# A gated mix of linear attention and expert lookup on one core: the subtracted feature and key moved to the end, one copy's order changed, and the seam, tile 5 and the drain put in another order

## The chip, the cores and the metric

The kernel is one program on one core of a Trainium2 chip. The core has a matrix engine (TensorE, PE; its weight loads are shown apart as PEld), a vector engine (VectorE, DVE), an activation engine (ScalarE, ACT), a general engine (GpSimd, POOL) and a queue engine (SyncE, SP), each with its own instruction queue worked off in order. They meet through semaphores. SBUF is the working memory of 128 partitions, PSUM the memory in which products are summed, in banks of 128 x 512 32-bit numbers. POOL does not read PSUM in this kernel. The metric is the device time of one execution in microseconds (us), the median of several runs.

## The reference

For 2048 tokens x of width 512, the output is `g*a + (1-g)*b`, with `g = sigmoid(sum(x*gate_w))`.

```
# a: linear attention, 32 heads of 16, feature map = two softmaxes per head
q, k, v = split(x @ wqkv)
pq, pk  = per head: q @ w_phi, k @ w_phi                # 16 features a head
phi(p)  = concat(softmax(p), softmax(-p))               # 32 a head
a = (phi_q @ (phi_k^T v)) / (phi_q @ sum(phi_k) + 1e-6) @ wo
# b: per token and head the best of 16 x 16 = 256 experts
q1, q2 = halves of x @ w_q                              # 32 heads, 2 x 128
i1, i2 = argmax(q1 @ k1^T), argmax(q2 @ k2^T)           # 16 keys each
b = sum over heads of gelu(x . u[16*i1+i2]) * v[16*i1+i2]
```

All inputs are 32-bit floating point. Two facts are used by the kernel and by the change: a softmax over 16 features, and the choice of the largest of 16 scores, do not change when one and the same number is taken off all 16.

## The kernel before

**Numbers.** A 32-bit operand is split into a high part, rounded to the matrix engine's fp32r format, and a low part, the remainder. A full product is then three matrix products: high by high, high by low, low by high (`mm3`, lines 52 to 59). `act` mostly rounds, `dve` or `pool` forms the remainder.

**Tiles.** The tokens are 16 tiles of 128 (t = 0 to 15). The first third of the program works on the keys and values of all tiles, tile by tile up to 4 then in pairs up to 14 (lines 501 to 607), and in the same loop turns the weights for the expert scores into one matrix. Then comes a seam (lines 608 to about 1010) in which the query weights are folded and the sums over all tokens are finished. The rest goes through the tiles again for queries, masks and outputs (`turned(a)`, line 1025, a from 2 to 14), and ends in a drain written out by hand for the tiles a = 15, b = 14, z = 13 (from line 1168). `manual_schedule` is on: each engine runs its instructions in the order in which the lines below issue them, so moving a line moves its instructions in the queue of each engine that it uses. PSUM banks are four for products ("mm"), three for turned results ("tr"), one for sums ("acc").

**The feature and the key taken off.** `from_first` (line 61) takes the first of 16 features off the other 15 in `wphi`, and the first of 16 keys off the other 15 in `kk`, and sets the first to zero. Products with these weights have 32 zero columns of 512 (columns are ordered feature by feature, 32 heads each). After the first product of a sum, which writes all 512 columns, the others leave those 32 out: `live` (line 71) takes columns 32 to 511. The second half of the scores lies as two runs of 16 heads (`HALF_RUNS`), so `live_of` takes columns 16 to 255 of each run of 256.

**Score weights.** For each of eight blocks j, PE multiplies raw query weights and keys into PSUM (line 315). `score_planes` (line 318) copies the block into two planes of 16-bit halves (ACT, L320) and has SP transpose them by DMA (L322). `join_tp` (line 330) puts the two planes together again as 32-bit numbers in `tj` (ACT, L331), `join_high` rounds them into their places in `sh` (ACT, L342), `join_low` puts the remainder into `sl` (POOL, L345). A block has, per partition and per k, eight heads m of 16 keys e. `tj` holds them in the order k, m, e; `places` holds them in the order k, e, m. There is one buffer each for the planes, the transposed planes and `tj`, so a block's copy into `tj` waits until the block before has been read by L345.

**The seam.** ACT rounds the expert values into `eh` (L631); POOL forms the two remainders `el` (L636) after DVE's and ACT's work on the folded weights, then two more for the output weights (L639), and with that a chain begins that ends in the denominators `z` (L985, L986, L998, L999, L969, L970).

**Masks, counts and coefficients.** `best` marks the best key of each head on DVE, `turn_eq` (line 771) has the marks transposed by DMA (L774), `mid_mask` (line 822) multiplies them on PE into a bank; two tiles share one such call from tile 5 on. `count` (line 833) is a chain of 17 small DVE steps, taken one at a time by `step(t, n)`, that turns the masks into how often each expert was chosen; `drain(t)` takes all that are left. `coef` (line 873) multiplies the counts by the gated gelu values, on POOL for tiles up to 14, on DVE for tile 15 (L875).

**Outputs.** `mid_num` gives the numerators of tiles (64 small products a pair of tiles, L807), `num_hi` (ACT, L814) and `num_lo` (DVE, L820) split them. The coefficients of an expert are turned either by DMA (`c_planes`, then `c_join` with L887 and L891 on ACT), or in the drain by PE (`back_c`, L900 and L903); `back_cl` gives the remainder (L908). `back(t, n)` issues the next n of the 18 products of tile t's output: 8 with the numerators' high parts, 4 with the low parts (both L920), 4 with the coefficients' high parts and 2 with the low parts (both L927). `back_some` issues as many of the next tiles' as `due(a)` asks for. `store(t)` copies the finished bank to `ot` (ACT, L958) and sends it out (SP, L959).

Of the kernel before, what the change touches and what calls it, by code (L numbers as in the profile page):

```python
# [12 lines left out]
U16 = mybir.dt.uint16  # L13
# [7 lines left out]
P = 128  # L21
# [13 lines left out]
def mix_kernel(ctx, tc, xT, wqT, wkT, wv, wphi, wo, wq, kk, ug, ev, cst, out):  # L35
# [24 lines left out]

    def from_first(w):
        g = w.rearrange("p a (i f) -> p (a i) f", f=F)
        pool.tensor_tensor(g[:, :, 1:], g[:, :, 1:], g[:, :, 0:1].to_broadcast([P, 8, F - 1]), op=ALU.subtract)
        pool.memset(g[:, :, 0:1], 0.0)

    HALF_RUNS = (1, 2)

    def live_of(runs):
        return lambda a: a.rearrange("p (r c) -> p r c", r=runs)[:, :, H // runs:]

    live = lambda a: a[:, H:]
    heads = lambda a: a.rearrange("p (f h) -> p h f", f=F)
# [257 lines left out]
    def join_tp(j, tp, tj):  # L330
        act.copy(tj.bitcast(U16).rearrange("p (k n j) -> p j k n", j=2, n=P),  # L331
                 tp.rearrange("p (j k) n -> p j k n", j=2))

# [4 lines left out]

    by_key = lambda tj: tj.rearrange("p (k m e) -> p k e m", k=NK, e=F)

# [47 lines left out]
    act.dma_start(cs, cst)  # L388
    from_first(wp)
    from_first(kp.rearrange("p a b c -> p (a b) c"))  # L390
    x_split(1)
# [238 lines left out]
    for k in range(2):  # L630
        act.copy(eh[:, k, :], rawe[k])  # L631
    next(fq)
    k_exp(t)
    k_sum(t)
    for k in range(2):
        pool.tensor_tensor(el[:, k, :], rawe[k], eh[:, k, :], op=ALU.subtract)  # L636
    for k in range(2):
# [173 lines left out]
    def num_hi(t):  # L811
        oh, ol, o = st8[t]["o"]
        for q in range(2):
            act.copy(oh[:, 2 * q:2 * q + 2], o[q])  # L814
# [58 lines left out]
    def coef(t):  # L873
        e = st8[t]
        (pool if t < NT - 1 else dve).tensor_tensor(e["C"], e["C"], e["G"], op=ALU.mult)  # L875

# [69 lines left out]
    def back_some(n):  # L946
        nonlocal ran
        t, n = ran // 18, min(n, 18 - ran % 18)
        if n > 0:
            back(t, n)  # L950
            ran += n
            if ran % 18 == 0:
                store(t)
# [71 lines left out]
    def turned(a):  # L1025
# [25 lines left out]
        if a < 5:  # L1051
            if a == 2:
                front_s(n, 1)
            else:
                mid_num(z)
                num_hi(z)
            if a == 3:
                front_s(n, 1)
            if masks:
                mid_mask(*masks)  # L1060
            if a > 3:
                front_s(n, 1)
            soft_exp(a)
        else:
            front_s(n, 1)
            soft_exp(a)
            if nums:
                mid_num(*nums)
            if parted is not None:
                num_hi(parted)  # L1070
            if masks:
                mid_mask(*masks)
            back_some(due(a) - ran)
        gelu_out(b)
# [103 lines left out]
    c_join(z - 2)  # L1178
    back_cl(z - 2, pool)
    soft_sum(a, 0)  # L1180
    step(z)
# [22 lines left out]
    num_lo(z)  # L1204
    step(a, 4)
    back(z - 1, 8)
    back(z, 8)
    mid_num(b)
    gelu_rest(a)
    num_hi(b)  # L1210
    back(z - 1, 4)
    back(z, 4)
    num_lo(b)
    c_join(z - 1)
    back_cl(z - 1, pool)
    back_c(z)
    store(z - 3)
    gelu_in(a)
    gelu_act(a)
    store(z - 2)  # L1220
    gelu_out(a)
    back(z - 1, 6)
    back(b, 12)
    step(a, 4)
    back_cl(z)
    join(a)
    back(z, 3)
# [3 lines left out]
    store(z - 1)  # L1231
    store(z)
    drain(a)
    num_lo(a)
    coef(b)
    coef(a)
    end = mm_bank("end")
    ends = back_mm(a, bank=end)
    for _ in range(10):
        next(ends)  # L1240
# [3 lines left out]
    back_cl(a)  # L1244
    for _ in range(2):
        next(ends)
    back(b, 6)
# [62 lines left out]
```

## Time and profile before

| what | value |
|---|---|
| runs shown | 363.80, 363.85, 364.68 us |
| median | 363.85 us |
| the profiled execution | 364.19 us |
| its span, first to last instruction | 362.5 us |
| TensorE clock granted | 1.000 of full speed |
| busy: DVE, ACT, POOL | 319.0, 259.9, 210.8 us |
| DVE share of the chain that ended last | 14% |

Rows of the trace name an instruction by the line in the kernel that issued it (L345 is line 345), its engine, what it writes and reads, and its size as partitions x elements. Times in rows are microseconds from the start of the span. A number in square brackets is how long the engine stood idle just before, with the instruction that released it. In rows of groups, `x8 | 12.8, 1606` means eight instructions, 12.8 us in all, 1606 ns each on average; other rows give the shortest, the median and the longest of a group in ns. "PEld" rows are weight loads, which come one ahead of their product; the busy time of PE itself is modelled at its ends, so starts are the better measure.

### The profile page before, as it was taken

What the parts mean: (1) busy time and instruction counts of PE and PEld (TensorE: products, weight loads), DVE (VectorE), ACT (ScalarE), POOL (GpSimd) and SP (SyncE); (2) the same over time, 40 slices, a digit from 0 to 9 for tenths busy, and PEclk for the clock granted to TensorE, in tenths of its full rate; (3) what the DMA queues carried; (4) which work ended last, traced back from release to release, by engine and by line L of the source; (5) the groups of instructions that cost most, each with busy time, mean ns of one, the idle gap of its engine ahead of it and who ended that gap; (6) DMA issues with size and microseconds to landing.
All of it is one profiled execution on the core that took longest, in us unless ns stands there. A gap on an engine that the chain in (4) does not pass through costs nothing.

```text
span 362.5 us, 8632 instructions
## 1 busy us (share of the span) xinstructions
PE 353.7 (98%) x3404; PEld 281.8 (78%) x3404; DVE 319.0 (88%) x639; ACT 259.9 (72%) x455; POOL 210.8 (58%) x209
## 2 busy tenths in 40 slices
PE   7999999999999999999999999999999999999995
PEld 3776667768778878888888788888888888888764
DVE  3769999999968879999999799899989899799891
ACT  4486588868666675695955976777768887767872
POOL 1169988989839957536445564654644645636230
PEclk9999999999999999999999999999999999999999
DMA  7869898367576121340552642653344255145233
GB/s 252 311 243 318 175 305 267 84 280 245 186 288 115 52 84 32 60 100 17 117 82 64 118 88 44 89 97 80 73 101 101 48 117 100 48 91 128 31 101 118
DMA packets 75752, 47.57 MB, mean 131 GB/s; under 512 B 67264, under 2 KB 68160, under 8 KB 73408
## 3 DMA queue, kind: packets, MB, share of 16 engines
q1 hardware_dynamic: 74848, 46.15, 48.7%
q10 hardware_dynamic: 864, 0.87, 0.9%
q8 instruction: 27, 0.44, 0.5%
q14 instruction: 13, 0.11, 0.1%
HBM read 26.43 MB, written 4.19 MB: 84 GB/s over the span
## 4 chain that ended last, share of the span: by engine, by line
PE 53%; POOL 14%; DVE 14%; ACT 8%; issue 6%; DMA 3%; SPq 0%; POOLq 0%; ACTq 0%; DVEq 0%
PE po L920 7%; PE s L57 4%; PE s L59 4%; PE s L58 4%; PE po L927 4%; PE pu L492 3%; PE pk L492 3%; POOL d L299 3%; PE pq L57 2%; PE pq L58 2%; PE pq L59 2%; PE ws L315 2%; PE oT L807 2%; DMA rawv<-wv 2%; ACT ptb L799 1%
## 5 line engine op out<-in xcount | busy, mean ns | idle before, releaser
L753 POOL TENSOR_TENSOR d<-d,st 128x512 f32<-128x512 f32 x30 | 32.8, 1114 | 46.3 <-DVE st L746 45.1
L724 POOL TENSOR_TENSOR w<-d,zb 128x512 f32<-128x512 f32 x32 | 41.5, 1318 | 18.0 <-ACT d L718 17.9
L57 PE MATMUL s<-sh,xh 128*128 128x480 f32 (+1 forms) x128 | 49.5, 387 | 0.0
L58 PE MATMUL s<-sl,xh 128*128 128x480 f32 x128 | 48.6, 380 | 0.0
L59 PE MATMUL s<-sh,xl 128*128 128x480 f32 x128 | 48.6, 380 | 0.0
L788 ACT COPY pl<-d 128x1024 uint16<-128x1024 uint16 x32 | 33.2, 1044 | 20.7 <-POOL d L753 20.7
L799 ACT COPY ptb<-tp 128x1024 uint16<-128x1024 uint16 x32 | 41.7, 1369 | 0.5 <-DMA tp<-pl 0.5
L299 POOL TENSOR_TENSOR d<-d,st 128x1024 f32<-128x1024 f32 x16 | 32.5, 2034 | 7.7 <-ACT d L290 6.0
L875 POOL TENSOR_TENSOR cf<-cf,px 128x256 f32<-128x256 f32 x15 | 11.0, 738 | 32.9 <-DVE cf L871 32.9
L57 PEld LDWEIGHTS s<-sh,xh 128*128 128x128 f32 x128 | 24.0, 187 | 4.4 <-issue 0.4
L59 PEld LDWEIGHTS s<-sh,xl 128*128 128x128 f32 x128 | 24.0, 187 | 4.3
L58 PEld LDWEIGHTS s<-sl,xh 128*128 128x128 f32 x128 | 24.0, 187 | 3.8
L57 PE MATMUL pq<-wah,xh 128*128 128x512 f32 (+1 forms) x64 | 24.6, 385 | 0.0
L179 DVE TENSOR_TENSOR xl<-xr,xh 128x512 fp32r<-128x512 f32 (+2 forms) x17 | 22.9, 1362 | 1.8 <-ACT xh L175 1.7
L58 PE MATMUL pq<-wal,xh 128*128 128x480 f32 x64 | 24.4, 381 | 0.0
L59 PE MATMUL pq<-wah,xl 128*128 128x480 f32 x64 | 24.3, 380 | 0.0
L728 DVE TENSOR_REDUCE st<-d 128x32 f32<-128x512 f32 x32 | 20.5, 678 | 3.6 <-ACT d L718 3.5
L769 DVE TENSOR_TENSOR eq<-s,mx 128x512 bf16<-128x512 f32 x32 | 22.1, 691 | 1.1
L767 DVE TENSOR_REDUCE mx<-s 128x32 f32<-128x512 f32 x32 | 21.8, 681 | 0.0
L732 DVE TENSOR_REDUCE st<-w 128x32 f32<-128x512 f32 x32 | 20.5, 676 | 0.9 <-POOL w L724 0.9
L294 DVE TENSOR_REDUCE st<-d 128x64 f32<-128x1024 f32 x16 | 19.4, 1210 | 1.8 <-ACT d L290 1.6
L958 ACT COPY ot<-po 128x512 f32<-128x512 f32 x15 | 8.7, 589 | 14.8 <-PE po L927 13.3
(275 smaller groups left out, 1103.1 us busy)
## 6 DMA issues: line engine op xcount, KB each, us to landing
wq<-wq SPq DMA_DIRECT2D x16, 1024.0 KB, 6.0
xr<-xT SPq DMA_DIRECT2D x15, 256.0 KB, 5.2
y<-ot SPq DMA_DIRECT2D x15, 256.0 KB, 2.0
rawk<-wkT SPq DMA_DIRECT2D x1, 1024.0 KB, 6.6
rawq<-wqT SPq DMA_DIRECT2D x1, 1024.0 KB, 6.8
rawu<-ug SPq DMA_DIRECT2D x2, 258.0 KB, 5.3
rawv<-wv ACTq DMA_DIRECT2D x2, 256.0 KB, 4.8
rawv<-wv SPq DMA_DIRECT2D x2, 256.0 KB, 6.0
```

The costliest lines, as they stand in the source:

```text
L57: pe.matmul(f(o), ah, f(bh), start=whole, stop=False, skip_group_check=True)
L58: pe.matmul(live(o), ah, live(bl), start=False, stop=False, skip_group_check=True)
L59: pe.matmul(live(o), al, live(bh), start=False, stop=(last and i == n - 1), skip_group_check=True)
L179: dve.tensor_tensor(l[:, ks], rawx[t][:, ks], h[:, ks], op=ALU.subtract)
L299: pool.tensor_tensor(g64(d), g64(d), b64(st[:, 128:192]), op=ALU.mult)
L724: pool.tensor_tensor(hs(e["w"], i), hs(e["ph"], i), hs(zb, i), op=ALU.mult)
L753: eng.tensor_tensor(g64(d)[:, gs_], g64(d)[:, gs_], r[:, gs_].unsqueeze(2).to_broadcast([P, 32, F]), op=ALU.mult)
L767: dve.tensor_reduce(m3, p4, axis=AX.X, op=ALU.max)
L769: dve.tensor_tensor(eq, p4, m4, op=ALU.is_equal)
L788: act.copy(pl, e["ph"][:, halves[i]].bitcast(U16).rearrange("p (c j) -> p j c", j=2))
L799: act.copy(p16[:, t % 2, :, 4 * i:4 * i + 4, :], st8[t]["tp"][i].rearrange("p (j g) n -> p j g n", j=2))
L920: pe.matmul(po, a, b, start=(i == 0), stop=False)
```

## The change

Seven things are altered; the results are the same up to rounding.

1. The last feature and the last key are taken off the others instead of the first (`from_last`), so the zero columns are the last ones. `live` becomes columns 0 to 479, and `live_of` columns 0 to 239 of each run of 256.
2. `join_tp` writes `tj` in the order k, e, m in place of k, m, e. It reads in order and writes every 16th 16-bit element, where it wrote every second one; L342 and L345 now read `tj` in order, where they read every 16th number.
3. One of the two remainders `el` goes from POOL to DVE and stands ahead of the last part of folding the query weights.
4. `coef` of tile 14 goes from POOL to DVE.
5. For tile 5 alone, the output products that stood behind the masks stand before them.
6. In the drain, stores, joins, activations, count steps and products are put in another order; in particular tile 10's store moves up by many lines, tile 12's coefficients are joined earlier, tile 15's two halves are joined one by one and earlier, tile 11's store stands ahead of tile 13's transposes, and tile 14's numerators are followed by more count steps.
7. All twelve products of tile 15 with the numerators stand before the last transposes, where two stood behind them.

```
-    def from_first(w):
+    def from_last(w):
         g = w.rearrange("p a (i f) -> p (a i) f", f=F)
-        pool.tensor_tensor(g[:, :, 1:], g[:, :, 1:], g[:, :, 0:1].to_broadcast([P, 8, F - 1]), op=ALU.subtract)
-        pool.memset(g[:, :, 0:1], 0.0)
+        n = F - 1
+        pool.tensor_tensor(g[:, :, :n], g[:, :, :n], g[:, :, n:].to_broadcast([P, 8, n]), op=ALU.subtract)
+        pool.memset(g[:, :, n:], 0.0)
...
-        return lambda a: a.rearrange("p (r c) -> p r c", r=runs)[:, :, H // runs:]
-    live = lambda a: a[:, H:]
+        return lambda a: a.rearrange("p (r c) -> p r c", r=runs)[:, :, :(D - H) // runs]
+    live = lambda a: a[:, :D - H]
...
     def join_tp(j, tp, tj):
-        act.copy(tj.bitcast(U16).rearrange("p (k n j) -> p j k n", j=2, n=P),
-                 tp.rearrange("p (j k) n -> p j k n", j=2))
+        act.copy(tj.bitcast(U16).rearrange("p (k e m j) -> p j k m e", j=2, k=NK, e=F),
+                 tp.rearrange("p (j k) (m e) -> p j k m e", j=2, e=F))
...
-    by_key = lambda tj: tj.rearrange("p (k m e) -> p k e m", k=NK, e=F)
+    by_key = lambda tj: tj.rearrange("p (k e m) -> p k e m", k=NK, e=F)
...
         act.copy(eh[:, k, :], rawe[k])
+    dve.tensor_tensor(el[:, 0, :], rawe[0], eh[:, 0, :], op=ALU.subtract)
     next(fq)
     k_exp(t)
     k_sum(t)
-    for k in range(2):
-        pool.tensor_tensor(el[:, k, :], rawe[k], eh[:, k, :], op=ALU.subtract)
+    pool.tensor_tensor(el[:, 1, :], rawe[1], eh[:, 1, :], op=ALU.subtract)
...
     def coef(t):
...
-        (pool if t < NT - 1 else dve).tensor_tensor(e["C"], e["C"], e["G"], op=ALU.mult)
+        (pool if t < NT - 2 else dve).tensor_tensor(e["C"], e["C"], e["G"], op=ALU.mult)
...
+            if a == 5:
+                back_some(due(a) - ran)
             if masks:
                 mid_mask(*masks)
-            back_some(due(a) - ran)
+            if a != 5:
+                back_some(due(a) - ran)
...
     back_cl(z - 2, pool)
+    store(z - 3)
...
-    step(a, 4)
+    step(a, 6)
     back(z - 1, 8)
     back(z, 8)
+    back(z - 1, 4)
     mid_num(b)
-    gelu_rest(a)
+    c_join(z - 1)
+    back_cl(z - 1, pool)
     num_hi(b)
-    back(z - 1, 4)
     back(z, 4)
     num_lo(b)
-    c_join(z - 1)
-    back_cl(z - 1, pool)
+    gelu_rest(a)
+    gelu_in(a)
+    back(z - 1, 6)
+    store(z - 2)
+    join_half(a, 0)
     back_c(z)
-    store(z - 3)
-    gelu_in(a)
+    join_half(a, 1)
     gelu_act(a)
-    store(z - 2)
     gelu_out(a)
-    back(z - 1, 6)
     back(b, 12)
-    step(a, 4)
+    step(a, 3)
     back_cl(z)
-    join(a)
     back(z, 3)
     mid_num(a)
     num_hi(a)
     back(z, 3)
     store(z - 1)
     store(z)
+    step(a, 7)
+    num_lo(a)
     drain(a)
-    num_lo(a)
     coef(b)
     coef(a)
     end = mm_bank("end")
     ends = back_mm(a, bank=end)
-    for _ in range(10):
+    for _ in range(12):
         next(ends)
     back_c(b)
     back_c(a)
     back_cl(b)
     back_cl(a)
-    for _ in range(2):
-        next(ends)
     back(b, 6)
```

4 lines of the change are left out of this document (2 added, 2 removed).

## The prediction

> **What bounds the kernel now.** I read the page's busy line first, then the chain that ended last, then the matrix engine's weight loads in order of time, because a load that stands idle before it shows where that engine really waited (columns: start us, duration, engine, line, operation; in the bracket the idle time before it and its releaser).
>
> ```profile
> span 362.5 us, 8632 instructions
> PE 353.7 (98%) x3404; PEld 281.8 (78%) x3404; DVE 319.0 (88%) x639; ACT 259.9 (72%) x455; POOL 210.8 (58%) x209
> PE 53%; POOL 14%; DVE 14%; ACT 8%; issue 6%; DMA 3%; SPq 0%; POOLq 0%; ACTq 0%; DVEq 0%
> 49.65 0.19 PEld L492 LDWEIGHTS pu<-uh,xl 128*128 128x128 f32 x1 [0.69 <-POOL xl L212]
> 61.68 0.19 PEld L492 LDWEIGHTS pe<-t1h,gl 128*128 128x128 f32 x1 [0.91 <-POOL gl L212]
> 75.13 0.19 PEld L492 LDWEIGHTS pe<-t1h,gl 128*128 128x128 f32 x1 [0.67 <-POOL gl L212]
> 79.88 0.16 PEld L315 LDWEIGHTS ws<-wq,kp 128*32 128x32 f32 x8 [0.80 <-DMA wq<-wq]
> 133.59 0.19 PEld L970 LDWEIGHTS z<-zl,neg 128*128 128x128 f32 x1 [0.54 <-DVE zl L999]
> 202.08 0.27 PEld L829 LDWEIGHTS <-et 128*128 128x128 bf16 x8 [0.63 <-DMA et<-eq]
> 345.43 0.19 PEld L927 LDWEIGHTS po<-eh,ch 128*128 128x128 f32 x1 [0.57 <-ACT ch L891]
> 347.17 0.19 PEld L920 LDWEIGHTS po<-t1h,xh 128*128 128x128 f32 x1 [0.32 <-DVE cl L908]
> 351.47 0.18 PEld L807 LDWEIGHTS oT<-ptb,kvb 64*32 64x32 f32 x16 [0.50 <-ACT ptb L799]
> 355.80 0.19 PEld L927 LDWEIGHTS po<-eh,ch 128*128 128x128 f32 x1 [0.21 <-ACT ch L903]
> ```
>
> PE is busy 98% of the span and holds 53% of the last chain, so a gain must come from PE's remaining waits, from the time of a product, or from the ends. Between 205 and 335 us no load of PE waits for data at all: a gain made before that stage reaches the end only if the other engines follow. The waits left are: three for POOL's differences in the stage of key tiles (49.65 to 75.13), one there for query weights from HBM (79.88), one for the denominators at the seam (133.59), one for a transposed mask (202.08), and four in the drain. A bracket overstates the loss by the time that the product before it still streams, about 0.23 us for a full product.
>
> The time of the profiled execution is 364.19 us, 1.7 us of it around the span; the median of the runs shown is 363.85. The sum below is a difference, so I take it off the median.
>
> **The joining copy (L331) and the two steps that read it (L342, L345).** Eight times, ACT puts the two 16-bit planes of a transposed weight block together (L331), rounds it (L342), and POOL forms the remainder (L345). Today L331 writes 2-byte elements 4 bytes apart, and the two readers step 64 bytes. The change makes the readers contiguous and gives L331 a write step of 32 bytes.
>
> ```profile
> L331 ACT COPY wtj<-wtp 128x1024 uint16<-128x1024 uint16 x8 | 11.0, 1370 | 3.0 <-POOL sl L345 1.9 <-POOL xr L198 1.1
> L342 ACT CAST sh<-wtj 128x512 fp32r<-128x512 f32 x8 | 8.9, 1107 | 1.1 <-PE pk L492 1.0
> L175 ACT CAST xh<-xr 128x512 fp32r<-128x512 f32 x13 | 7.7, 624 | 0.6 <-PE pv L492 0.6
> L788 ACT COPY pl<-d 128x1024 uint16<-128x1024 uint16 x32 | 33.2, 1044 | 20.7 <-POOL d L753 20.7
> L345 POOL TENSOR_TENSOR sl<-wtj,sh x8: 1534/1554/2008, 40.4 to 120.3; 128x512 fp32r<-128x512 f32 x8
> L636 POOL TENSOR_TENSOR el<-rawe,eh 128x512 fp32r<-128x512 f32 x2 | 2.6, 1302 | 0.0
> ```
>
> L175 is L342's work without the step: L342 should fall from 1107 to 624 ns, 0.48 us. L636 is L345's without it: 1554 (its median) to 1302, I take 0.26 us. For L331 no row shows the new write. Against L788, the same copy with a contiguous write, today's 4-byte write step costs (1370 - 1044)/1024 = 0.32 ns an element; L342's 64-byte read step costs (1107 - 624)/512 = 0.94. Lower end: the wider step costs no more, 1.37 us. Upper end: today's price plus L342's whole extra, 1.37 + 1024 x 0.94 = 2.34 us. Between lies a plain copy with L342's extra alone, 1.04 + 0.97 = 2.01 us. The nearest row is L331's own; I charge its present extra once more: 1.37 + 0.33 = 1.70 us. So the copy is w = 0.33 us longer, between 0 and 0.97.
>
> The Trainium skill, "Advanced Engine Details and Errata", section "SBUF Cachelines", says that SBUF has lines of 16 bytes and that an access pattern needs two hits on a line to run at full rate; by it the new write (one hit a line) pays, and the old one (four) does not. The trace bears out half of it: L342 (one hit a line) pays, but L331 pays already with four. By the rule alone the copy would take about the 2.01 us above, and the sum below would be -0.8 us.
>
> Where this meets the path:
>
> ```profile
> 50.64 1.24 SPq L322 DMA_TRANSPOSE wtp<-wpl  x1
> 55.28 1.37 ACT L331 COPY wtj<-wtp 128x1024 uint16<-128x1024 uint16 x1 [1.11 <-POOL xr L198]
> 56.75 0.57 ACT L576 COPY pk<-pu 128x512 f32<-128x512 f32 x1
> 59.62 0.64 ACT L206 CAST gh<-xr 128x512 fp32r<-128x512 f32 x1
> 64.62 1.37 ACT L331 COPY wtj<-wtp 128x1024 uint16<-128x1024 uint16 x1 [1.90 <-POOL sl L345]
> 70.84 1.01 SPq L166 DMA_DIRECT2D wq<-wq  x2
> ```
>
> PE's wait at 49.65 is for a POOL difference with one L345 ahead of it in POOL's queue: PE gains 0.26 there. That does not last. The copy before 50.64 runs w longer, so the transpose of the next block goes out w later, the copy that waits for them (55.28, end 56.65) starts w later and ends 2w later; L576 follows it after 0.1 us, and ACT then runs without a gap, L342 among it, to L206 at 59.62. POOL's difference from that and PE at 61.68 so move by 2w - 0.1 - 0.48. L345 takes 0.26 off before the next copy at 64.62 (it waits for just that L345), the copy adds w, its L342 takes 0.48: the next planes, and behind them on SP's queue the loads of wq at 70.84, move by 3w - 1.32. PE waits for one of these loads at 79.88, so the stage hands on 3w - 1.32. At 75.13 POOL is earlier too (another 0.26), which this last wait covers. After it the loads of wq follow PE's own pace. With w = 0.33: **-0.3 us**; at the ends -1.3 and +1.6.
>
> **Last feature and key instead of first (from_last, live).** The same instructions, the same shapes: POOL's two subtractions and memsets are moved to other columns. The short products now run over columns 0 to 479, or two runs of 240 from 0 and 256, instead of starting at 32 (or 16). This is on the path only if a product's time depends on where its run begins:
>
> ```profile
> 324.73 0.38 PE L58 MATMUL pq<-wal,xh 128*128 128x480 f32 x1
> 326.91 0.38 PE L59 MATMUL pq<-wah,xl 128*128 128x480 f32 x1
> ...
> 327.12 0.28 PE L57 MATMUL pp<-uh,xh 128*128 128x258 f32 x1
> 328.44 0.29 PE L59 MATMUL pp<-uh,xl 128*128 128x258 f32 x1
> ...
> 340.27 0.39 PE L920 MATMUL po<-t1h,xh 128*128 128x512 f32 x1
> 341.40 0.39 PE L920 MATMUL po<-gl,xh 128*128 128x512 f32 x1
> ```
>
> From start to start: 480 columns 2.18/10 = 0.218 us, 258 columns 1.32/11 = 0.120, 512 columns 1.13/5 = 0.226. A line through the last two gives 0.213 at 480: the short products, the only ones of the three that don't begin at 0, take some 5 ns more than their length asks for. They might owe that to their start, or to their length. I take 0 in the forecast and carry the other as a rival. A loss has no reason: the products of 512 start at 0 too.
>
> **The seam: one of two remainders from POOL to DVE.**
>
> ```profile
> 124.59 1.28 POOL L639 TENSOR_TENSOR t1l<-rawo,t1h 128x512 fp32r<-128x512 f32 x1 [0.29 <-ACT t1h L638]
> 121.62 2.48 DVE L237 TENSOR_TENSOR wal<-foldq,wah 128x512 fp32r<-128x512 f32 x4 [1.10 <-ACT wah L236]
> ```
>
> POOL is 1.3 us (L636) earlier with its second remainder, but the next step, L639, waits for ACT's t1h anyway (bracket 0.29), and ACT for its earlier work on the folded weights. So POOL idles longer and PE's wait at 133.59, at the end of that chain, stays: 0 us. On DVE the step has L237's bracket, 1.10 us, for cover. Were that cover gone, L237 would be late by the step's own length, which on POOL is 1.3 us at most, and PE's first use of its result (tile 0's pq) comes some 4 us after L237 begins.
>
> **Tile 5: output products ahead of the masks.**
>
> ```profile
> 199.28 2.76 DMA et<-eq
> ...
> 202.45 1.26 PE po L920 x5
> 203.71 1.36 PE po L927 x6
> ```
>
> Of 16 mask products, eight wait for tile 5's transposed mask, landing at 202.04. Now the 11 output products (2.6 us) go first; only the last two need the cl that DVE makes meanwhile. The mask has landed when they end. PE's bracket of 0.63 goes, less a change of shape: **-0.55 us**. What comes later is the count that reads the masks; its first step stands on DVE behind tile 5's sums and one `best`, some 4 us on. Afterwards PE meets no wait until 335; whether the 0.55 passes rests on DVE, which itself waits for PE's pq four times in that stage, so it can follow; if not, 0.
>
> **The drain.** PE's order becomes: twelve products of tile 12 and eight of 13, tile 14's numerators, four of 13, six of 12, the transposes of 13, twelve of 14, three of 13, tile 15's numerators, three of 13, twelve of 15, the transposes of 14 and 15, six of 14, six of 15.
>
> ```profile
> 344.02 0.76 DVE L820 TENSOR_TENSOR xl<-oT,xh 128x256 fp32r<-128x256 f32 x2 [1.30 <-ACT xh L814]
> 344.15 0.79 ACT L887 COPY ctj<-tpc 128x512 uint16<-128x512 uint16 x1
> 353.22 0.58 DVE L875 TENSOR_TENSOR cf<-cf,px 128x256 f32<-128x256 f32 x1
> 354.73 0.59 PEld L900 LDWEIGHTS CT<-cs,cf 128*128 128x128 f32 x4
> ```
>
> Removed: tile 12's join (L887, then ch) moves ahead of three activations and two conversions on ACT, from 344.15 to some 342.6, so ch and POOL's cl are ready before PE arrives (bracket at 345.43, some 0.45 lost). Tile 11's store moves ahead of tile 13's transposes, so tile 14's sums find a free bank and no longer wait for cl of 13 (347.17: 0.17). Tile 15's two joins come before gelu's activations, done at some 349.1, and PE is there at 349.9: no wait between its halves (351.47: 0.4). Tile 10's store moves into ACT's wait for tile 12's numerators, before 335.5, and its DMA on SP stands 4 us clear of the next transpose there.
>
> Added: the twelve products of tile 15 now all stand before the transposes. From L900's load (354.73) to tile 14's first correction product (355.80) are 1.07 us, covered before by four transposes and two products; now only by the transposes: some 0.55 of wait where 0.21 stood. In products of 0.228 from 338.45 on, PE reaches the transposes of 14 at 354.1, and the corrections begin at 355.0 against 355.86: **-0.85 us**. The DVE has to hold that: six count steps instead of four fill its 1.30 us bracket at 344.02, but it now does tile 14's coefficients too (0.58, L875), after the last count step, in line with tile 15's. With each step as long as before it ends the remainders of 14 at 344.9, three count steps and cl of 13 (behind ACT's ch, 347.8) at 348.2, seven steps at 351.6, the remainders of 15 at 352.3, the last step at 353.0, and the two coefficients at 353.5 and 354.05, some 0.5 us before they would cost. A few count steps slowed by POOL would use that up. Bounds: -1.1 (no new wait) and 0 (DVE 0.9 late).
>
> **Sum:** -0.3 + 0 + 0 - 0.55 - 0.85 = -1.7 us: 363.85 - 1.7 = 362.15, forecast 362.2; with every term at its better or its worse end (tile 5: -0.6 to 0) 360.9 to 365.4.
>
> **Rivals.**
> (1) The start of a run counts. 528 of the short products (352 into s, 176 into pq) run from 116 us on, where PE does not wait; at 5 ns each they give 2.6 us, with the forecast's terms 359.5. For it: the 5 ns stand out wherever I looked. Against: starts at 32 and at 16 columns cost about the same. The Trainium skill, "TensorE: Matmul & The Clock Gate", section on the back-to-back issue gap, has a gap of columns over the clock plus a fixed 2.5 ns, wherever the run starts; by it this rival gives nothing. The trace's fixed parts are larger than that and not even: 13 ns at 512 columns, 18 at 480 by the same clock.
> (2) The copy is dear: the other side. At 2.34 us (w = 0.97) the weights stage gives +1.6, and with the other terms 363.85 + 0.2 = 364.0; the change is slower than before once L331 takes 2.28 us, and by over 0.3% (1.1 us, about what a measurement of this kernel tells from no change) from 2.64 us. For it: three copies in series before the loads at 70.84. Against: the only stepped write in the trace that pays at all is L331's own, with 0.32 ns.
> (3) The copy takes L342's rate, 2.02 us: the stage gives +0.65, the sum is -0.75: 363.1.
> (4) DVE ends the drain: its coefficients come 0.9 us late, the drain gives nothing: 363.0.
>
> **Chances.** Forecast (361.4 to 362.7) 0.35; (1) 0.20; (3) 0.14; (4) 0.15; (2) 0.16, of which 0.12 over 0.3%. Faster by over 0.3% (under 362.75): 0.55; within 0.3%: 0.14 + 0.15 + 0.04 = 0.33; slower: 0.12. The range runs from (1) to the first part of (2): 359.6 to 364.4, leaving out some 0.15.
>
> **What would show it.** Right: L331 near 1.7, L342 near 0.62, L345 near 1.3 us; no bracket before the masks of tile 5; none at the six corrections of tile 12 or between tile 15's numerators, and about 0.5 before those of tile 14; 133.59's bracket still there. Wrong: 480 columns start to start at 0.213 (rival 1); a copy above 2 us, with longer brackets at 61.68 and 79.88 (2, 3); the drain's transposes waiting for L875 (4); or new waits between 205 and 335.

## The result, and the profile after

The changed kernel takes 375.58 us (median of four runs, 375.32 to 375.89) where the kernel before, beside it, takes 363.95. The ratio is 1.0316, with a 95% interval from 1.0298 to 1.0334. The forecast was 362.2 us, the range 359.6 to 364.4: the change makes the kernel 3.2% slower, and the prediction is wrong in sign and size. The profiled execution took 375.89 us. (Lines in the changed kernel stand one higher than before from line 66 on: the joining copy is now L332, its readers are L343 and L346.)

The page's busy line and its chain that ended last, changed kernel:

```profile
span 374.1 us, 8631 instructions
PE 356.8 (95%) x3404; PEld 283.9 (76%) x3404; DVE 319.2 (85%) x641; ACT 281.2 (75%) x455; POOL 206.6 (55%) x207
...
PE 68%; ACT 9%; POOL 8%; DMA 7%; DVE 3%; issue 3%; SPq 0%; ACTq 0%; POOLq 0%
```

PE fell from 98% to 95% of a longer span. ACT's share of the chain is hardly larger (9% for 8%), but the page's list of the chain by lines now has the loads of wq with 5% and the joining copy L332 with 4%, which the list of before does not have. The page's second part shows one slice of PE at 4 tenths and the digits of the clock at 7 and 8 there, which before were at 9. PE's weight loads in the changed kernel's timeline, with the idle time before each in brackets, say where (all of 0.8 us or more between 42 us and the drain):

```profile
47.58 0.19 PEld L493 LDWEIGHTS pe<-t1h,gl 128*128 128x128 f32 x1 [1.08 <-DVE gl L213]
52.88 0.16 PEld L316 LDWEIGHTS ws<-wq,kp 128*32 128x32 f32 x8 [1.35 <-DMA wq<-wq]
63.33 0.29 PEld L493 LDWEIGHTS pk<-sh,xh 128*128 128x128 f32 x1 [5.48 <-ACT pk L577]
79.61 0.19 PEld L493 LDWEIGHTS pk<-sh,xh 128*128 128x128 f32 x1 [1.19 <-ACT pk L577]
88.12 0.16 PEld L316 LDWEIGHTS ws<-wq,kp 128*32 128x32 f32 x8 [1.38 <-DMA wq<-wq]
114.75 0.16 PEld L316 LDWEIGHTS ws<-wq,kp 128*32 128x32 f32 x8 [1.46 <-DMA wq<-wq]
122.87 0.19 PEld L59 LDWEIGHTS pk<-wah,xl 128*128 128x128 f32 x1 [1.57 <-DVE xl L180]
134.16 0.19 PEld L58 LDWEIGHTS s<-sl,xh 128*128 128x128 f32 x1 [0.87 <-POOL sl L346]
145.54 0.19 PEld L970 LDWEIGHTS z<-zh,neg 128*128 128x128 f32 x1 [1.07 <-ACT zh L999]
```

One wait of 5.48 us is new, for ACT's copy L577, which stands right behind a joining copy in ACT's queue:

```profile
58.28 4.52 ACT L332 COPY wtj<-wtp 128x1024 uint16<-128x1024 uint16 x1 [2.43 <-DMA wtp<-wpl]
62.32 0.96 ACT L577 COPY pk<-pu 128x512 f32<-128x512 f32 x1
```

The groups of the three lines of the joining step (count, us in all, ns each; the last row gives shortest, median and longest):

```profile
L332 ACT COPY wtj<-wtp 128x1024 uint16<-128x1024 uint16 x8 | 37.3, 4662 | 3.2 <-DMA wtp<-wpl 2.4
L343 ACT CAST sh<-wtj 128x512 fp32r<-128x512 f32 x8 | 4.9, 618 | 1.1 <-PE pk L493 1.0
L346 POOL TENSOR_TENSOR sl<-wtj,sh x8: 1280/1296/1753, 39.5 to 132.8; 128x512 fp32r<-128x512 f32 x8
```

The two readers came out as predicted (618 ns for 624, a median of 1296 for 1302). The copy did not: 4.66 us, 3.4 times its 1.37 before, where the prediction took 1.70 and 2.34 at most. The windows of the changed kernel (length; busy time of PE, PEld, DVE, ACT, POOL with their instructions; granted clock) show what the long wait did on top:

```profile
62.00:67.00 5.00, 3.67 (x9) 2.93 (x10) 1.65 (x3) 5.00 (x8) 1.18 (x1) 0.50 0.23 44
82.00:116.00 34.00, 32.75 (x449) 23.31 (x450) 28.01 (x42) 30.13 (x29) 24.55 (x25) 1.00 0.67 239
```

After the idle 5.48 us PE was granted half its clock: a full product took some 0.4 us from start to start instead of 0.22. The Trainium skill, "TensorE: Matmul & The Clock Gate", Part 1 on the clock gate, says that the clock falls to half after an idle window of about 3.4 us; the trace agrees with its 5.48 us and its 0.50. What this clock cost in the end is taken up below.

### The profile page after: what moved, and what is told of

It reads as the page before. It is cut to its first block, busy times and chain, and to the rows that moved or that the text cites. A ratio compares the mean times of both kernels' runs of the same rounds, so it can differ in the third digit from the quotient of the medians.

```text
span 374.1 us, 8631 instructions
## 1 busy us (share of the span) xinstructions
PE 356.8 (95%) x3404; PEld 283.9 (76%) x3404; DVE 319.2 (85%) x641; ACT 281.2 (75%) x455; POOL 206.6 (55%) x207
## 4 chain that ended last, share of the span: by engine, by line
PE 68%; ACT 9%; POOL 8%; DMA 7%; DVE 3%; issue 3%; SPq 0%; ACTq 0%; POOLq 0%
PE po L921 11%; PE s L57 7%; PE s L58 7%; PE s L59 7%; PE po L928 6%; DMA wq<-wq 5%; ACT wtj L332 4%; PE pq L57 4%; PE pq L59 3%; PE pq L58 3%; PE oT L808 2%; PE pp L57 2%; PE pp L58 2%; PE pp L59 2%; PE pu L493 2%
## 5 line engine op out<-in xcount | busy, mean ns | idle before, releaser
L300 POOL TENSOR_TENSOR d<-d,st 128x1024 f32<-128x1024 f32 x16 | 31.1, 1941 | 16.2 <-DVE st L296 16.2
L332 ACT COPY wtj<-wtp 128x1024 uint16<-128x1024 uint16 x8 | 37.3, 4662 | 3.2 <-DMA wtp<-wpl 2.4
L180 DVE TENSOR_TENSOR xl<-xr,xh 128x512 fp32r<-128x512 f32 (+2 forms) x17 | 19.5, 1164 | 3.5 <-ACT xh L176 3.4
```

Of the source, the lines that this page charges most:

```text
L300: pool.tensor_tensor(g64(d), g64(d), b64(st[:, 128:192]), op=ALU.mult)
L332: act.copy(tj.bitcast(U16).rearrange("p (k e m j) -> p j k m e", j=2, k=NK, e=F), tp.rearrange("p (j k) (m e) -> p j k m e", j=2, e=F))
```

## The experiments

Two theories stood at the start. **The copy:** the whole loss comes from L332, and the other parts gain what the forecast gave them. **The rest:** some of it lies in the other parts, the seam above all, since a bracket of 1.07 us stands before the denominators (145.54), where before had 0.54. This table is worked out from the traces: how much later than in the kernel before the same weight loads start (median over the timeline's rows of loads in a stretch of before's time, us). The difference in the stretch 20 to 42, which each run has from its start (-0.1 to -0.7), is taken off. Where nothing was changed the rows repeat to some hundredths of a microsecond (`e6`, `e7`). In the rows after, e2 and e9 the stretch 57 to 60 lies behind the long wait, and its single loads run from about +6 to +8.

```
stretch of before   57-60  81-91 107-110 112-116 138-145 207-215 300-335 356.5-358.5
after               +6.75  +8.68  +10.01  +11.45  +13.14  +12.51  +12.35  +11.42
e1  old copy        +0.06  +0.21   +0.26   +0.27   +0.21   -0.35   -0.52   -1.45
e2  new copy only   +6.60  +8.39   +9.69  +11.14  +12.87  +12.88  +12.88  +12.85
e3  loops exchanged -0.21  -0.10   -0.06   -0.04   -0.07   -0.69   -0.85   -1.78
e5  last, only      +0.05  +0.13   +0.24   +1.74   +1.71   +1.72   +1.56   +1.55
e6  tile 5 only     +0.02  +0.04   +0.03   +0.03   +0.04   -0.54   -0.54   -0.53
e7  drain only      +0.01  -0.07   -0.07   -0.07   -0.05   -0.05   -0.05   -1.00
e8  seam only       -0.02  +0.18   +0.22   +0.22   +0.23   +0.21   +0.22   +0.17
e9  blocks 0-2      +6.54  +5.90   +5.92   +5.92   +5.94   +5.89   +5.90   +5.87
e10 blocks 3-7      -0.03  +2.82   +4.05   +5.50   +8.77   +8.42   +8.43   +8.40
e11 half            +1.50  +2.62   +2.72   +4.22   +4.43   +3.73   +3.56   +2.63
e12 best            -0.20  -0.30   -0.25   +0.13   +0.09   -0.55   -0.72   -1.64
```

### The copy alone, and everything but the copy

`e1` puts the copy's order back in the changed kernel, `e2` puts the new order into the kernel before:

```
 e1, from the changed kernel
-        act.copy(tj.bitcast(U16).rearrange("p (k e m j) -> p j k m e", j=2, k=NK, e=F),
-                 tp.rearrange("p (j k) (m e) -> p j k m e", j=2, e=F))
+        act.copy(tj.bitcast(U16).rearrange("p (k n j) -> p j k n", j=2, n=P),
+                 tp.rearrange("p (j k) n -> p j k n", j=2))
...
-    by_key = lambda tj: tj.rearrange("p (k e m) -> p k e m", k=NK, e=F)
+    by_key = lambda tj: tj.rearrange("p (k m e) -> p k e m", k=NK, e=F)
```

> The changed kernel with the joining copy's order, and the order in which its two readers step, put back; every other part of the change stays. Theory 1 (the joining copy is the whole loss, and the other parts gain what the forecast gave them): the copy is back at 1.37 us, the 5.48 us wait of PE is gone, and the time is 362.3 us (361.7 to 362.9), about 1.5 below the kernel before. Theory 2 (a part of the loss lies in the other parts, the seam above all, where the trace shows PE's bracket before the denominators grow from 0.54 to 1.07 us): above 363.9 us.

> The kernel before with the new order of the joining copy alone. Theory 1 (the copy is the whole loss): the copy takes about 4.68 us each time and the kernel 377.1 us, that is 1.5 more than the changed kernel, whose other parts gain. Theory 2 (other parts lose as well): 375.5 us or less.

Measured: `e1` 363.11 us against 364.59 for the kernel before on that chip (0.9949, interval 0.9931 to 0.9967); `e2` 377.00 us (1.0332, 1.0307 to 1.0356). The copy is the whole loss. (`e1` lies a little above the 361.7 to 362.9 that were expected, as the kernel before lies above its 363.85 on that chip; the difference of 1.5 us is the expected one.) The long bracket before the denominators is the copy's doing too: `e2` has it (1.04 us, on ACT's zh) without the new seam, and `e1`, with the new seam, has only the 0.54. The table's first and third rows run together within 0.35 us up to the denominators.

### The same placement with the loops exchanged

```
-        act.copy(tj.bitcast(U16).rearrange("p (k e m j) -> p j k m e", j=2, k=NK, e=F),
-                 tp.rearrange("p (j k) (m e) -> p j k m e", j=2, e=F))
+        act.copy(tj.bitcast(U16).rearrange("p (k e m j) -> p j k e m", j=2, k=NK, e=F),
+                 tp.rearrange("p (j k) (m e) -> p j k e m", j=2, e=F))
```

> The changed kernel with the loops of the joining copy exchanged: the same elements go to the same places, but eight successive 2-byte writes now lie 4 bytes apart before the step of 32 bytes, and the 32-byte step goes to the reading side. Theory 1 (a write that enters a new stretch of 16 bytes is what costs, some 4.4 ns each, and a reading step costs as L343's did before the change, 0.94 ns an element): the copy takes 1.4 to 2.4 us and the kernel 361 to 363.5. Theory 2 (the permutation itself costs, by its number of loops): the copy stays above 4 us and the kernel at 375.6. Theory 3 (a step of 32 bytes between 2-byte elements costs on whichever side it stands): the same, above 4 us.

The copy in `e3` (shortest, median, longest in ns):

```profile
L332 ACT COPY wtj<-wtp x8: 2196/2267/2305, 33.6 to 116.0; 128x1024 uint16<-128x1024 uint16 x8
```

2.27 us, and 362.81 us for the kernel (0.9943, 0.9922 to 0.9965): theory 1. The same bytes go to the same places, so neither the permutation nor a 32-byte step as such is dear; a 32-byte step between successive 2-byte writes is. And a copy 0.9 us longer than before cost nothing in the end: more on that below.

### What a write costs, by its step

`e4` adds copies behind the last output of the kernel before, into a buffer `W` (`W4` seen as 4-byte elements) no longer read. `src` is contiguous.

```
+    step = lambda a, n, s: a[:, :n * s].rearrange("p (n s) -> p n s", s=s)[:, :, 0]
...
+    act.copy(W[:, :384], src)                # L1262
+    act.copy(step(W, 384, 2), src)           # L1263: every 2nd, 4th, 8th, 16th to L1266
...
+    act.copy(W[:, :384], step(R, 384, 2))    # L1267: reading every 2nd, 8th, 16th to L1269
...
+    act.copy(step(W4, 384, 2), src4)         # L1271: 4-byte elements, every 2nd, 4th, 8th to L1273
...
+    act.copy(W[:, :6144].rearrange("p (n s) -> p n s", s=16)[:, :, :2], ...)   # L1274: pairs
+    act.copy(W[:, :2048].rearrange("p (n s) -> p n s", s=16)[:, :, :8], ...)   # L1275: runs of eight
+    act.copy(... "p (k e m j) -> p j k m e" ...)   # L1276: the change's order
+    act.copy(... "p (k e m j) -> p j k e m" ...)   # L1277: loops exchanged
...
+    dve.tensor_copy(step(W, 384, 16), src)   # L1282
+    dve.tensor_copy(... "p (k e m j) -> p j k m e" ...)   # L1283
+    dve.tensor_copy(... "p (k n j) -> p j k n" ...)       # L1284: before's order
```

> The kernel before with 26 copies added behind its last output, one after another, into a buffer that is no longer used; nothing is left out, and only the duration of each added copy is read, not the kernel's time. ACT, 384 elements a partition, per element after about 0.19 us of fixed time. Theory 1 (each write that enters a new stretch of 16 bytes costs some 4.4 ns): 2-byte elements at a step of 2 bytes 1.0 ns or less, at 4 bytes 1.2, at 8 bytes 2.2, at 16 and at 32 bytes 4.4; pairs of adjacent elements every 32 bytes 2.2; runs of eight every 32 bytes about 1; 4-byte elements the same by their steps, 4.4 at 16 and 32 bytes; reading steps at most 2. Theory 2 (only a step of 32 bytes costs): 4 to 16 bytes 1.0 to 1.3, 32 bytes 4.4. Theory 3 (a 2-byte write that does not complete a longer word costs): 8, 16 and 32 bytes all near 4.4, pairs near 1, 4-byte elements near 1 at every step.

From the timeline of `e4` (start, duration in us; one execution, each copy once):

```profile
361.23 0.51 ACT L1262 COPY ptb<-sl 128x384 uint16<-128x384 uint16 x1 [0.42 <-ACT ot_end L1254]
361.77 0.62 ACT L1263 COPY ptb<-sl 128x384 uint16<-128x384 uint16 x1
362.42 1.04 ACT L1264 COPY ptb<-sl 128x384 uint16<-128x384 uint16 x1
363.49 1.89 ACT L1265 COPY ptb<-sl 128x384 uint16<-128x384 uint16 x1
365.41 1.79 ACT L1266 COPY ptb<-sl 128x384 uint16<-128x384 uint16 x1
367.24 0.51 ACT L1267 COPY ptb<-sl 128x384 uint16<-128x384 uint16 x1
367.78 0.86 ACT L1268 COPY ptb<-sl 128x384 uint16<-128x384 uint16 x1
368.67 0.88 ACT L1269 COPY ptb<-sl 128x384 uint16<-128x384 uint16 x1
370.12 0.53 ACT L1271 COPY ptb<-sl 128x384 f32<-128x384 f32 x1
370.69 0.86 ACT L1272 COPY ptb<-sl 128x384 f32<-128x384 f32 x1
371.58 0.88 ACT L1273 COPY ptb<-sl 128x384 f32<-128x384 f32 x1
372.50 0.88 ACT L1274 COPY ptb<-sl 128x768 uint16<-128x768 uint16 x1
373.41 1.04 ACT L1275 COPY ptb<-sl 128x1024 uint16<-128x1024 uint16 x1
374.48 4.47 ACT L1276 COPY ptb<-sl 128x1024 uint16<-128x1024 uint16 x1
378.99 2.04 ACT L1277 COPY ptb<-sl 128x1024 uint16<-128x1024 uint16 x1
385.19 2.31 DVE L1283 COPY ptb<-sl 128x1024 uint16<-128x1024 uint16 x1
387.53 0.74 DVE L1284 COPY ptb<-sl 128x1024 uint16<-128x1024 uint16 x1
```

The 384 contiguous elements and the 1024 in runs of eight give (1.04 - 0.51)/640 = 0.83 ns an element and 0.19 us fixed. With that off, a 2-byte write costs 1.12 ns at a step of 4 bytes, 2.2 at 8, 4.4 at 16 and 4.2 at 32. Counted by the stretches of 16 bytes that are entered, the four are one price: 4 x 1.12 = 4.5, 2 x 2.2 = 4.4, 4.4, 4.2 ns a stretch. That is theory 1 for 2-byte elements. For 4-byte elements and for adjacent pairs theory 1 was wrong: a stretch costs them only 1.7 to 1.8 ns (0.86, 0.88 us for 384), as it does the 2-byte reads (L1268, L1269). So a stretch of 16 bytes costs about 1.8 ns, and 4.4 where single halves of 4-byte words are written: theory 3's condition, at theory 1's price per stretch. Why single halves cost more is not shown. DVE pays half as much for the change's order (2.31 us), with a like leap from before's (0.74).

The two copies follow: 0.19 us + 1024 x 4.4 ns = 4.7 us for the change's order, a stretch for each element; 0.19 + 1024 x 1.12 = 1.34 for before's, four to a stretch. With the loops exchanged, reading enters a stretch each time: 0.19 + 1024 x 1.8 = 2.03, and the writes at 4 bytes hide under it (measured 2.04 in `e4`, 2.27 in `e3`).

The Trainium skill, "Advanced Engine Details and Errata", section "SBUF Cachelines", which the prediction weighed, has lines of 16 bytes and full rate from two hits a line on. The reads and the 4-byte writes here agree (0.53 us at 8 bytes against 0.51 contiguous, 0.86 at 16). The 2-byte writes do not: with two hits they take 1.04 us, twice the contiguous time, with four still 0.62.

### Each other part by itself

`e5` to `e8` put one part each into the kernel before: the last feature and key; tile 5; the drain; the seam.

> The kernel before with the last feature and key taken off instead of the first, and nothing else. Theory 1 (a product does not care where its run of columns starts): no difference, within 0.3 us of the kernel before on the same chip; products of 480 columns stay 0.218 us from start to start. Rival (the start of a run costs 5 ns, rival 1 of the prediction): 0.213 us each and 2.6 us less for the kernel.

> The kernel before with the eleven output products of tile 5 ahead of its masks, and nothing else. Theory 1 (the step gives what the forecast gave it, and PE carries it to the end): 0.55 us less than the kernel before on the same chip (0.3 to 0.8), and no bracket for the mask's landing. Rival (the gain is lost later, PE waiting where it did not): 0.

> The kernel before with the new order of the drain, the coefficients of tile 14 on DVE and the earlier stores, and nothing else. Theory 1 (the step gives what the forecast gave it): 0.85 us less than the kernel before on the same chip (0.6 to 1.1), the waits of PE at 345.43, 347.17 and 351.47 gone and one of about 0.5 us before the corrections of tile 14. Rival (DVE with its added coefficients ends the drain): 0 to 0.3 less, and the transposes before the corrections wait for L875.

> The kernel before with one of the two remainders at the seam moved from POOL to DVE, and nothing else. Theory 1 (the forecast's 0): no difference, within 0.3 us of the kernel before on the same chip, and the bracket of 0.54 us before the denominators stays. Rival (the longer bracket there in the changed kernel is this step's doing): 0.5 us more, a bracket of 1.07 us on ACT's zh.

The times hardly tell these from the kernel before, and only `e8`'s interval leaves out 1: ratios of 1.0006 (0.9988 to 1.0024), 0.9992 (0.9977 to 1.0008), 0.9986 (0.9967 to 1.0005) and 1.0020 (1.0003 to 1.0037). The table can. Tile 5 gives -0.58 us and PE carries it to the end. The drain gives -0.95. The seam gives nothing: +0.23 before it and +0.21 behind it. The last key gives almost nothing: -0.15 between 145 and 195, given back at about 200, and -0.16 little by little between 215 and 335. Products of 480 columns stand 0.217 us from start to start in `e5` (326.11 to 328.28, ten products), not at the rival's 0.213.

The tell-tale rows of the drain, `e7`, and of the seam, `e8` (PE's loads):

```profile
354.63 0.19 PEld L927 LDWEIGHTS po<-eh,ch 128*128 128x128 f32 x1 [0.48 <-ACT ch L903]
```

```profile
133.35 0.19 PEld L970 LDWEIGHTS z<-zl,neg 128*128 128x128 f32 x1 [0.54 <-DVE zl L999]
```

Both are as forecast: about 0.5 us of wait before tile 14's corrections, and the 0.54 before the denominators unchanged. The 0.7 us by which `e8`'s times lie above the kernel before are not found at the seam; in its profile the last instruction is issued 0.3 us earlier than before and the span ends 0.3 us later, behind the last store. What does that stays open.

### Times in two groups

The medians above are blurred because several of these kernels have two groups of times 1.7 us apart: the kernel before, beside `e5`, has 28 runs at 363.5 to 364.5 and 7 at 365.2 to 366.0. `e5`'s profile fell into the upper group (365.56 us), and the table puts its loss between 110 and 112 us. Timelines of `e5` and then of the kernel before, which fell into the lower:

```profile
113.44 0.19 PEld L59 LDWEIGHTS pk<-wah,xl 128*128 128x128 f32 x1 [1.65 <-DVE xl L180]
...
110.91 2.47 DVE L180 TENSOR_TENSOR xl<-xr,xh 128x512 fp32r<-128x512 f32 x1 [0.22 <-ACT xh L176]
...
110.90 1.94 POOL L300 TENSOR_TENSOR d<-d,st 128x1024 f32<-128x1024 f32 x1
```

```profile
110.85 0.69 DVE L179 TENSOR_TENSOR xl<-xr,xh 128x512 fp32r<-128x512 f32 x1 [0.21 <-ACT xh L175]
...
110.91 2.44 POOL L299 TENSOR_TENSOR d<-d,st 128x1024 f32<-128x1024 f32 x1
```

DVE's remainder of tile 15 and POOL's product start within 0.1 us of each other. If DVE is first it takes 0.69 us and POOL waits (2.44 for 1.94); if POOL is first, by 10 ns here, DVE takes 2.47 and PE waits 1.65. The Trainium skill, "SBUF — State Buffer", section "SBUF: two separate sides", describes it: of a DVE instruction with two SBUF operands and a GpSimd one, whichever starts first holds their shared ports for its whole length. The trace agrees nearly: the later one ends 0.54 us (DVE) or 1.81 us (POOL) after the earlier one, some 0.15 us less than the 0.69 and 1.94 that each takes alone. The profiles fit the groups: of the kernels with two groups, POOL is first in `e5` and `e11`, whose profiled times lie in the upper one, and DVE in the kernel before and in `e6` to `e8`, in the lower. In the changed kernel POOL is first, by 90 ns, and the 1.57 us at 122.87 are this.

`e12` takes the race away, on top of `e3`:

```
         if t == NT - 3:
-            x_split(NT - 1)
+            x_high(NT - 1)
+            h, l = x_of(NT - 1)
+            pool.tensor_tensor(l, rawx[NT - 1], h, op=ALU.subtract)
```

> The changed kernel with the loops of the joining copy exchanged and tile 15's remainder formed by POOL, ahead of its product with the softmax, instead of by DVE beside it. Theory 1 (the second group of times, 1.7 us above the first in nearly every kernel here, is DVE's remainder of 0.69 us held for 2.47 us when POOL's instruction starts some 10 ns ahead of it): all runs in one group, at 362.8 us as with the exchanged loops alone, none above 363.6. Rival (POOL's queue, 1.3 us longer, comes out at the denominators): 363.4 us or more, with a longer bracket there.

Measured: 362.41 us, nine runs from 361.83 to 362.85, against 363.83 for the kernel before (0.9957, 0.9942 to 0.9973). No run lies in an upper group, as with `e1` and `e3` (eleven runs), where DVE happened to be 20 to 30 ns ahead in the profile. In its profile PE waits 0.51 us for POOL there (111.41), and the table shows 0.4 us lost. `e12` beats both kernels, but it can't be told from `e3`, and since those eleven runs have no upper group either, it doesn't show that the group is gone for good.

### How 3.3 us a copy become 12

> The kernel before with the new order of the joining copy for the first three of the eight weight blocks alone (the copies at 33.80, 48.05 and 55.28 in the trace of before). Theory 1 (the chain that the prediction named: three copies in series ahead of the loads of wq, 3w - 1.32 with w = 3.3 us): 8.6 us above the kernel before on the same chip (7.5 to 9.5), with PE's wait of some 5.5 us near 63 us. Rival (ACT as a whole is too full, and every copy costs alike): three eighths of the 13 us of all eight, 4.9 us.

> The kernel before with the new order of the joining copy for the last five of the eight weight blocks alone. Theory 1 (the chain of the first three carries most of the loss): 3.7 us above the kernel before on the same chip (2.5 to 4.5), in several waits of PE between 75 and 125 us, none above 2 us. Rival (every copy costs alike): five eighths of the 13 us, 8.1 us.

```
     def join_tp(j, tp, tj):
-        act.copy(tj.bitcast(U16).rearrange("p (k n j) -> p j k n", j=2, n=P),
-                 tp.rearrange("p (j k) n -> p j k n", j=2))
+        if j < 3:                            # e10: j > 2
+            act.copy(tj.bitcast(U16).rearrange("p (k e m j) -> p j k m e", j=2, k=NK, e=F),
+                     tp.rearrange("p (j k) (m e) -> p j k m e", j=2, e=F))
+        else:
+            act.copy(tj.bitcast(U16).rearrange("p (k n j) -> p j k n", j=2, n=P),
+                     tp.rearrange("p (j k) n -> p j k n", j=2))
```

`e9` took 370.78 us (1.0197, 1.0166 to 1.0228), `e10` 371.60 (1.0204, 1.0178 to 1.0231): 7.0 and 7.8 us. Neither expectation was met, and an equal price per copy is out as well: `e10` lies near the 8.1 of that rival, but `e9` not near its 4.9. For `e9` the expectation was drawn up wrongly: the prediction's chain runs over blocks 1, 2 and 3, and block 0's copy is not in it, so only two of its three copies are in `e9`. Their part of it, 2w - 0.1 - 0.48 - 0.26 = 5.8 us, is what the table shows (5.90). Block 3 makes up the rest, w - 0.48 = 2.8: `e10` has +2.82 at 81 to 91, and the changed kernel 8.68 where the prediction's formula, 3w - 1.32, gives 8.6. The halved clock behind the long wait has no part in this: `e9` has the wait and the clock too (5.84 us, 0.50 from 60 to 66 us) and needs nothing beyond the formula, and in the changed kernel PE waits 1.38 us for the loads of wq at 88.12 all the same. (The table has `e9`'s profiled execution, 369.66 us, the fastest of four; what made the others 1.1 to 2.3 us slower is not known.)

What the prediction left out comes after that: "the loads of wq follow PE's own pace". They do not once a pair of tiles has 3.3 us more of ACT. The changed kernel loses 1.3 us in two more pairs (to 107-110), 1.4 in the race for tile 15's remainder, and 1.7 up to the denominators; `e10` shows the same steps. That ACT's longer copies are behind the first and the last of these is read from the waits there (for L577, wq, POOL's sl and ACT's zh), not shown by a run of its own.

`e10` adds another 1.6 behind the denominators (its loads fall back from +7.20 to +8.77), so that the two parts sum to more than the whole. The granted clock was halved there (columns as above):

```profile
136.00:141.00 5.00, 3.77 (x22) 2.55 (x21) 2.98 (x7) 2.68 (x8) 2.40 (x1) 1.00 0.24 52
141.50:144.50 3.00, 3.00 (x9) 2.52 (x8) 2.56 (x8) 2.22 (x7) 1.08 (x2) 0.50 0.01 3
145.00:150.00 5.00, 5.00 (x30) 4.46 (x29) 4.25 (x10) 1.58 (x6) 3.44 (x4) 1.00 0.25 56
```

Products of 480 columns stand 0.40 us apart in the second window. No bracket of PE in the stretch before it is above 1.10 us, far from the idle window named above, and the changed kernel keeps its clock at 1.00 with nearly the same brackets (145.54 and behind). Why it fell stays open.

> The changed kernel with the joining copy in two: the low halves in the new order, the high halves with the loops exchanged. By the table the first takes 512 x 4.4 + 190 ns = 2.4 us and the second about 1.2 us, together 3.6, which is w = 2.2 over the kernel before. Theory 1 (the chain of the prediction, 3w - 1.32, from the 363.1 us of the version with the old copy): 368.4 us, up to 369.5 with later waits. Theory 2 (nothing up to 2.27 us, where the exchanged loops cost nothing, then evenly up to the 375.6 us at 4.68): 369.9 us. Theory 3 (evenly from the old copy's 1.37 us on): 371.5 us.

```
+        for h, order in enumerate(("p k m e", "p k e m")):
+            w = tj.bitcast(U16).rearrange("p (k e m j) -> p j k m e", j=2, k=NK, e=F)[:, h]
+            r = tp.rearrange("p (j k) (m e) -> p j k m e", j=2, e=F)[:, h]
+            act.copy(w.rearrange("p k m e -> " + order), r.rearrange("p k m e -> " + order))
```

`e11` took 365.54 us (1.0039, 1.0019 to 1.0059; of ten runs one was 878.95, for no known reason, one 367.38, the others 364.96 to 365.73). All three theories were too high, in part because the second half begins 0.5 us before the first has ended: together 3.2 us, w = 1.8. The formula gives 3 x 1.8 - 1.32 = +4.1, the table +2.62 at 81 to 91. For `e3` it gives 3 x 0.9 - 1.32 = +1.4, the table -0.10. So it is 1.5 us too high at both, and right at w = 3.3. Where the 1.5 went is seen between the issue of block 2's transpose on SP and the copy that waits for it, in `e1`, `e3` and the changed kernel (whose copy is shown above, at 58.28):

```profile
49.86 1.24 SPq L323 DMA_TRANSPOSE wtp<-wpl  x1
...
54.70 1.37 ACT L332 COPY wtj<-wtp 128x1024 uint16<-128x1024 uint16 x1 [1.19 <-DMA wtp<-wpl]
```

```profile
50.75 1.26 SPq L323 DMA_TRANSPOSE wtp<-wpl  x1
...
54.34 2.26 ACT L332 COPY wtj<-wtp 128x1024 uint16<-128x1024 uint16 x1 [0.58 <-DMA wtp<-wpl]
```

```profile
53.38 1.24 SPq L323 DMA_TRANSPOSE wtp<-wpl  x1
```

From issue to copy it is 4.8 us in `e1`, 3.6 in `e3`, 3.1 in `e11` (52.31 to 55.45) and again 4.9 in the changed kernel. The transpose does not land a fixed time after its issue: at the two middle lengths of the copy 1.2 to 1.7 us of the delay were made up there, at the full length nothing. The DMA queues are busy with loads at that time (a share of 0.89 from 45 to 62 us in `e1`); that these loads set the landing is a guess, and no run tests it.

## Why the prediction was wrong, point by point

**The joining copy: the step that failed.** The prediction put L331 at 1.70 us, "1.37 + 0.33", between 1.37 and 2.34, and the upper end was "today's price plus L342's whole extra". It measured 4.66. The upper end took the price of a 4-byte read (1.8 ns a stretch in `e4`) for that of a 2-byte write (4.4). The right number could be had from the rows quoted there: L331 writes 1024 elements in 256 stretches of 16 bytes, (1370 - 190)/256 = 4.6 ns each, and the change makes them 1024. The prediction saw that L331 "pays already with four" and read 0.32 ns an element in it, where a price per stretch was the other reading. By that, 0.19 + 1024 x 4.6 ns = 4.9 us and rival 2 far beyond its 2.64. (The 190 ns are `e4`'s, but two rows quoted there nearly give them: L887 writes 512 elements in the same way in 0.79 us, L331 1024 in 1.37, so 1.13 ns an element and 0.21 us fixed.) Nor was L331 "the only stepped write in the trace that pays at all": L799, which joins halves in the same way 32 times, takes 1369 ns for 1024 elements on the page of before.

**Rival 2, the dear copy**, was the right one, with 0.16 of the chance. Its place for PE's wait was only in part right: of the two brackets that were to grow, 79.88's did (1.38 us at 88.12), 61.68's went, and the 5.48 us stand one step earlier, where PE needs the result of the copy right behind the joining copy (L576 there, at 56.75, L577 now). The prediction passed through that copy on ACT and put no wait of PE at it. Its point was wrong too: it was to be slower from 2.28 us on, and `e3` at 2.27 us is 0.6% faster than before. By `e11` and `e3` it lies between 2.3 and 3.2 us.

**The chain through 55.28 and 64.62** was named rightly, and its formula holds at the measured w (8.6 for 8.68), though it is 1.5 us too dear at 0.9 and 1.8. What was missing is the further loss behind the loads of wq, 4.5 us up to the denominators. The prediction's list of waits leaves out one of the kernel before that bears on it:

```profile
105.07 0.29 PEld L315 LDWEIGHTS ws<-wq,kp 128*32 128x32 f32 x8 [0.57 <-DMA wq<-wq]
```

PE waited for wq there already, so these loads had nothing to spare; in the changed kernel the wait is 1.46 us (114.75).

**The last feature and key**: 0 was right to a third of a microsecond (-0.15 and -0.16, the first given back). Rival 1 had the sign but not the 2.6 us.

**The seam**: 0, as predicted, in the trace; its times stay unexplained. **Tile 5**: -0.55 predicted, -0.58 in `e6`. **The drain**: -0.85 predicted, -0.95 in `e7`, with the predicted wait of about 0.5; rival 4 did not come. In the changed kernel the two are the same (table: -0.63 with a little of the last key, and -0.93). `e1`, all of the change but the copy, measures 1.5 us less than before, where the terms without the copy sum to -1.4.

## What to carry to other kernels

Price a strided copy by the stretches of 16 bytes that it enters, on the reading and on the writing side, and by whether it writes whole 4-byte words: a reader saved 0.5 us here and the writer paid 3.3. When an order must change, let the wide step fall on the reading side and keep successive 2-byte writes close together (2.27 us against 4.66 for the same bytes). And where no row shows an operation, try each unit (element, stretch, instruction) on the rows there are before a bound is drawn.

## What was unexpected of the hardware

A 2-byte write at a 4-byte step is the cheap end of a price per 16 bytes, not a surcharge per element (`e4`). Waits of 5.48 to 5.84 us halved the clock of PE in three runs (the changed kernel, `e2`, `e9`), which made full products 0.4 us long for some 4 us and cost nothing in the end that the profiles show, since PE still waited later for the loads of wq; in `e10` the clock was halved for some 3 us without a wait above 1.10 us, and that cost 1.6. And 10 ns in which of two engines starts first were worth 1.65 us of PE's time, in a kernel whose times otherwise repeat within about 1 us.
